# Loading the fourth pair of token tiles by quarters, and three last output transfers from another queue

## The chip, the cores and the metric

The kernel runs on one core of a Trainium2 chip. The metric is the device time of one execution in microseconds (us). Five engines work side by side, each in its own program order: TensorE (PE, with its weight loads as PEld), VectorE (DVE), ScalarE (ACT), GpSimd (POOL) and SyncE (SP). DMA transfers are issued here by SP and by ScalarE, each through a queue of its own (SPq and ACTq in the profile).

## The reference, cut to what matters

```python
a = softmax(phi)                                  # per head, over 32 memory slots
k_m, v_m = a^T k, a^T v
x = softmax(q k_m^T / 8) v_m                      # (2304, 512) after joining the heads
x = ((x @ w_a) * (x @ w_b)) @ w_out               # first MLP, d_ff = 1536
h = x @ w_in                                      # second MLP, (2304, 2048)
g = h * sigmoid(1.702 * h)
out = g @ w_out2                                  # (2304, 512), float32
```

The change touches only the last product, `out = g @ w_out2`, and the transfer of `out` to DRAM.

## The kernel before

The tensor `g` is not kept on the chip: each finished piece goes to a DRAM scratch tensor `g2d` (2048 by 2304, the contraction first) and comes back in the order that the last product wants. That product runs over nine pairs of token tiles (`NW = 9`, 256 tokens a pair). The contraction of 2048 is 16 chunks of 128; a quarter is `K4 = 4` chunks.

**Splitting.** Every operand is split into a high part and a low part, and a product is three matmul passes. A loaded piece of `g` of one token tile and one quarter (128 by 512) is split by one ACT copy (line 308) and one subtraction on DVE or POOL (line 302, `combine`). The result is a block in one of the six `sb_s` slots; in the profile the blocks are `attn` and the loaded pieces are `acc`. PE takes a block in 12 matmuls (line 1335) and with that frees the slot. The chunks of the weight are the `wo2` tiles, which the profile names by the buffers in which they lie (`wv`, `whl_a`, `y`, `g`, `whl_b`, `eff_b`).

**The front.** Pairs 0 to 2 (`NF = 3`) are the front. Their pieces come by quarters, one DMA of 512 KB for one pair and one quarter, into six `f_s` slots (the last two of these are given when the last raw weights are requested). All three pairs advance together, quarter by quarter, over 24 blocks in six PSUM banks. Meanwhile the last rows of `w_out2` are still arriving as `raw` (line 334, SP queue) and are decoded: ACT line 417, DVE lines 419, 423, 427 and 432, ACT line 448 and `combine`. DVE's line 432 frees the `raw` slot for the next load.

**Pairs 3 and 4** (`NS = 5`) follow one after the other, eight blocks each, in quarter order. Their pieces come by halves, one DMA of 1024 KB (line 1204) into one of three `fw_s` slots. These three wide slots lie over the same memory as the six `f_s` slots: the first over the two given last, the second over two others, the third over the remaining two. Two of them are given at the mark `front`, when the last quarter piece has been split, and the third once a block of pair `NF`'s second half has been split. So the halves of pair 3 can't be loaded before the front's last pieces in that memory have been split.

**Pairs 5 to 8** are computed with seven products instead of eight (line 1366). They need combined weights (`blocks`), made between the blocks from pieces of `w2d` that the ACT queue loads (line 1298, two `tb_s` slots).

**The order.** A planner inside the kernel (`Order`) runs these steps as streams with priorities and assumed durations and thereby writes out a fixed order for each engine and each queue. An instruction that waits holds all that stands behind it on its engine. A slot is handed on when the planner emits the instruction that frees it.

**The output.** `store` sends one tile of 128 tokens as four DMAs of 64 KB (line 1417), all from SP. A pair of the last kind has two outputs: `o1` is stored after the product P4 is added, `o0` at the very end, after P3.

Of the kernel before, what the change touches and what calls it, by code (L numbers as in the profile page):

```python
# [56 lines left out]
def crowded():  # L57
    measured()
    Lengths.pool, Lengths.both, Lengths.slow = 1.3, 1.75, 1.55


def short():
    Lengths.dve, Lengths.act, Lengths.psum = 68, 94, 52
    Lengths.pool, Lengths.both, Lengths.slow = 1.0, 1.0, 1.0


def dve(n, fast=False):
    return Lengths.dve + n / (1.92 if fast else 0.96)


def act(n, psum=False):
    return (Lengths.psum if psum else Lengths.act) + n / 1.2
# [102 lines left out]
def tile_mem_attention_moe_moe2(  # L175
# [13 lines left out]
    nc = tc.nc  # L189
# [4 lines left out]
    NT, DM = out.shape  # L194
    F1 = w_o1.shape[0]
    F2 = w_o2.shape[0]
    P = 128
# [5 lines left out]
    QP = P // 4  # L203
# [13 lines left out]
    K4 = F2 // P // 4  # L217
    NB = 2 * P
# [93 lines left out]
    loaded = {}  # L312
# [415 lines left out]
    def give(slots_, views):  # L728
        slots_.free += [[x, now()] for x in views]
# [202 lines left out]
    win_s, hb_s, f_s, fw_s, sb_s, tb_s = Slots(), Slots(), Slots(), Slots(), Slots(), Slots()  # L932
    wo2_t, blocks = {}, []

    def views(m, n, count, o=0):
        return [m[:, o + i * n:o + (i + 1) * n] for i in range(count)]
# [79 lines left out]
    def room_chunks(*flat):  # L1016
        for x in flat:
            od.mark(now(), "room", "o2", len(wo2))
            wo2.append(x.rearrange("p (i f) -> p i f", i=2))
# [4 lines left out]
    def room_last():  # L1024

        short()
        od.handicap[DVE] = W1
        used = wt["o1", NG1 - 1][0]
        room_chunks(*views(g1_m, CN, 3), *views(used, CN, 2), *views(big["eff_b"], CN, 1))
        for x, o, n in (  # L1030
            (big["y0"], 0, 14), (big["y0"], 18 * DM, 3), (eff_m, 0, 4), (attn_m[0], 4 * SN, 1),
            (attn_m[1], 2 * SN, 5), (big["eff_b"], CN, 2), (p2_rest[0], 0, 4),
        ):
            blocks.extend(x.rearrange("p (i f) -> p i f", i=2) for x in views(x, BN, n, o))
        for q in order:
            for j in range(2):
                for u in range(2):
                    yield "mark", "g2", q, j, u
        n = KD * 2 * N2
        give(f_s, views(acc, FN, 1, n + 2 * FN))  # L1040
        give(tb_s, views(acc, 2 * DM, 2))
        for p in range(F2 // P // 2):
            od.spawn(PT, load_pair(p))
        for c, x in enumerate(views(acc, FN, 2, n), len(pieces) - 3):
            yield "mark", "raw", c
            give(f_s, [x])
        t = yield "mark", "wo2", F2 // P - 1
        crowded()
        od.mark(t, "decoded")
        yield "mark", "front"  # L1050
        wide = views(acc, 2 * FN, 3, n)
        give(fw_s, wide[:2])
        yield "mark", "sb", NF, 2 * K4, 0
        give(fw_s, wide[2:])
        for p in range(F2 // P // 2):
            yield "mark", "wt", p
        short()
        give(dm_s, views(acc, DM, 4))
# [133 lines left out]

    NF, NS, NW = 3, 5, NT // NB

    def gated_part(s, i, o, e):
        t = 0.0
        for g in range(o // G2, (e - 1) // G2 + 1):
            for n in range(i * NB // N2, ((i + 1) * NB - 1) // N2 + 1):  # L1200
                for j in range(2):
                    t = max(t, (yield "mark", "g2", (g, n // 2), j, n % 2))
        f = s[0].rearrange("p (c t) -> p c t", c=e - o)
        nc.sync.dma_start(
            out=f, in_=g2d[o * P:e * P, i * NB:(i + 1) * NB].rearrange("(c p) t -> p c t", p=P)
        )
        od.load(max(t + 2500.0, s[1]), 1.7 * (e - o) * P * NB * 4, "f", i, o)
        loaded["f", i, o] = s, f

    def load_gated():  # L1210
        for o in range(0, 4 * K4, K4):
            for i in range(NF):
                s = yield "slot", f_s
                yield from gated_part(s, i, o, o + K4)
        for i in range(NF, NW):
            for o in (0, 2 * K4):
                s = yield "slot", fw_s
                yield from gated_part(s, i, o, o + 2 * K4)

    def split_part(t, src, *key):  # L1220
        b = yield "slot", sb_s
        loaded[key] = b
        od.spawn(4, split_into(max(t, b[1]), b, src, key))

    def split_into(t, b, src, key):
        t = yield from hi_lo(t, b[0][:, HI], b[0][:, LO], src, K4 * P)
        od.mark(t, *key)

    def split_gated():
        for o in range(0, 4 * K4, K4):  # L1230
            for i in range(NF):
                t = yield "mark", "f", i, o
                slot, f = loaded.pop(("f", i, o))
                for s in range(2):
                    yield from split_part(t, f[:, :, s * P:(s + 1) * P], "sb", i, o, s)
                for s in range(2):
                    t = max(t, (yield "mark", "sb", i, o, s))
                f_s.release(slot, t)
        od.mark(t, "front")
        for i in range(NF, NW):  # L1240
            yield from (split_whole(i) if i < NS else sums_gated(i))

    def split_whole(i):
# [47 lines left out]
    def load_pair(p):  # L1291

        t = max((yield "mark", "w2d", 2 * p), (yield "mark", "w2d", 2 * p + 1))
        for x in blocks[4 * p:4 * p + 4]:
            wo2_t.setdefault(p, []).append(x)
        m = yield "slot", tb_s
        x = m[0].rearrange("p (k j f) -> p k j f", k=2, j=2)
        nc.scalar.dma_start(
            out=x.rearrange("p k j f -> p k (j f)"),
            in_=w2d[2 * p * P:(2 * p + 2) * P, :].rearrange("(k p) f -> p k f", p=P),  # L1300
        )
        od.load(max(t, m[1]), 2 * P * DM * 4, "pair", p)
        t = max((yield "mark", "pair", p), (yield "mark", "decoded"))
        b11, b12, b21, b22 = (x[:, k, j] for k in range(2) for j in range(2))
        n = DM // 2
        for i, (dst, in0, in1) in enumerate(
            ((b11, b12, b11), (b12, b22, b12), (b22, b22, b11), (b21, b21, b22))
        ):
            t = yield from combine(t, dst, in0, in1, ALU.subtract, n)
            od.spawn(PT, split_t(t, wo2_t[p][i], dst, p, i))  # L1310
        for i in range(4):
            t = max(t, (yield "mark", "wt", p, i))
        tb_s.release(m, t)
        od.mark(t, "wt", p)
# [61 lines left out]
    def sums_out(i, ps):  # L1376
        x = yield "slot", dm_s
        o0 = yield "slot", dm_s
        o1 = yield "slot", dm_s
        lo, hi = slice(0, NB), slice(NB, 2 * NB)  # L1380
        t = yield "mark", "done", i, "P1"
        t, _ = yield ACT, max(t, x[1]), act(NB, True)
        nc.scalar.activation(out=x[0][:, lo], in_=ps["P1"][0][:, :NB], func=AF.Copy)
        bank_m.release(ps["P1"], t)
        base = max(t, o0[1], o1[1])
        for name, dst, src, last in (
            ("P2", o0[0][:, lo], x[0][:, lo], True), ("P6", x[0][:, hi], x[0][:, lo], True),
            ("P7", x[0][:, lo], x[0][:, hi], True), ("P5", o0[0][:, hi], x[0][:, hi], False),
            ("P5", o1[0][:, hi], x[0][:, lo], True), ("P4", o1[0][:, lo], x[0][:, lo], True),
            ("P3", o0[0][:, hi], o0[0][:, hi], True),  # L1390
        ):
            t = yield "mark", "done", i, name
            base, _ = yield DVE, max(t, base), dve(NB)
            nc.vector.tensor_tensor(out=dst, in0=ps[name][0][:, :NB], in1=src, op=ALU.add)
            if last:
                bank_m.release(ps[name], base)
            if name == "P4":
                dm_s.release(x, base)
                store(2 * i + 1, o1[0])
                dm_s.release(o1, base + 4000.0)  # L1400
        store(2 * i, o0[0])
        dm_s.release(o0, base + 4000.0)

    def proj2_out(t, it, ps):
# [3 lines left out]
        store(it, m[0])  # L1408
        dm_s.release(m, t + 4000.0)

    def store(i, src):

        for t in range(i * P, (i + 1) * P, QP):
            b, r = divmod(t, S)
            e, c = divmod(r // QP, QC // 2)
            dst = out[b * S:(b + 1) * S, :].rearrange("(p c) e -> p c e", c=QC)
            nc.sync.dma_start(out=dst[:, 2 * c + e, :], in_=src[t - i * P:t - i * P + QP, :])

    order = [(0, 0), (1, 0), (0, 1), (1, 1), (0, 2), (1, 2)]
    order += [(g, p) for g in range(2, NG2 - 2) for p in range(NP)]  # L1420
# [11 lines left out]
    def main():  # L1432
# [75 lines left out]
        for i in range(3):  # L1508
            yield "mark", "dm_x", i
        room_projected()  # L1510
        od.spawn(6, load_gated())
        od.spawn(5, split_gated())
        for q in order[1:]:
# [74 lines left out]
```

## Time and profile before

| | |
|---|---|
| runs | 789.92, 791.01, 790.88 us; median 790.88 us |
| profiled execution | 790.42 us |
| its span (first to last instruction or transfer) | 788.6 us |
| granted TensorE clock, mean over the span | 0.996 |
| instructions | 14,299 |

The profiled execution has 1.8 us outside its span and lies 0.46 us below the median of the runs. In the rows below a line begins with its start in us and its length in us; "idle before" is how long the engine had stood and what released it. Matmul starts are reliable, their ends are modelled and overlap the next start.

### The profile page before, as it was taken

The numbers are of one execution on the slowest core, as the hardware profiler recorded it, in microseconds if no ns is written. First come the engines' busy times: TensorE is split into PE (matmuls) and PEld (weight loads), VectorE is DVE, ScalarE is ACT, GpSimd is POOL, SyncE is SP. The second block draws the span as 40 slices with busy tenths as digits, with TensorE's granted clock in tenths as the row PEclk, the third lists the DMA queues.
The fourth block names the chain that finished last, engine by engine and source line by source line (L and its number), as shares of the span: only waits on it lengthen the run. The fifth ranks groups of instructions, "written<-read, shape, count | busy, mean of one in ns | idle before, by whom it ended". The sixth has DMA issues, their size and how long they took to land.

```text
span 788.6 us, 14299 instructions
## 1 busy us (share of the span) xinstructions
PE 772.0 (98%) x5216; PEld 711.6 (90%) x5216; DVE 638.9 (81%) x1135; ACT 417.8 (53%) x925; POOL 365.2 (46%) x343
## 2 busy tenths in 40 slices
PE   8999999999999999999999999999999997999997
PEld 7777789999899899989999999999998885889997
DVE  4888978999999997977989778777867878547886
ACT  4567768564645655445565555555544445434442
POOL 1224225553645644436799655333341046453563
PEclk9999999999999999999999999999999998999999
DMA  8866400122213221230013545455598738624421
GB/s 297 311 190 196 148 25 28 55 81 81 81 54 108 81 81 53 72 90 1 1 65 101 183 159 172 149 164 174 208 309 271 226 135 257 215 75 134 135 81 28
DMA packets 70151, 103.96 MB, mean 132 GB/s; under 512 B 5824, under 2 KB 48832, under 8 KB 70080
## 3 DMA queue, kind: packets, MB, share of 16 engines
q1 hardware_dynamic: 64768, 93.84, 37.3%
q10 hardware_dynamic: 5312, 9.21, 3.3%
q8 instruction: 41, 0.67, 0.4%
q14 instruction: 30, 0.25, 0.1%
HBM read 75.24 MB, written 27.79 MB: 131 GB/s over the span
## 4 chain that ended last, share of the span: by engine, by line
PE 83%; DVE 5%; DMA 4%; ACT 3%; issue 2%; POOL 1%; ACTq 0%; POOLq 0%; DVEq 0%; SPq 0%
PE bank L1135 22%; PE bank L831 18%; PE bank L1366 10%; PE bank L864 10%; PE bank L887 9%; PE bank L1335 6%; PE bank L787 3%; DMA raw<-in_moe_w_out_dram 2%; PE bank L619 1%; PE bank L575 1%; DMA raw<-in_moe_w_b_dram 1%; DVE attn L302 1%; PE bank L756 1%; PE bank L494 1%; DMA acc<-w2d 1%
## 5 line engine op out<-in xcount | busy, mean ns | idle before, releaser
L1177 DVE TENSOR_TENSOR acc<-bank,acc 128x384 f32<-128x384 f32 x168 | 89.7, 553 | 31.8 <-PE bank L1135 20.2
L302 DVE TENSOR_TENSOR attn<-acc,attn 128x512 fp32r<-128x512 f32 (+1 forms) x93 | 88.0, 967 | 30.7 <-ACT attn L308 30.6
L302 POOL TENSOR_TENSOR acc<-acc 128x512 f32<-128x512 f32 (+2 forms) x59 | 76.2, 1306 | 55.7 <-DVE attn L302 30.5
L308 ACT ACTIVATE attn<-acc 128x512 fp32r<-128x512 f32 (+2 forms) x114 | 66.6, 603 | 62.4 <-PE bank L1366 18.7
L1187 ACT ACTIVATE acc<-acc 128x384 f32<-128x384 f32 x96 | 49.3, 523 | 53.1 <-DVE acc L1177 52.2
L844 ACT ACTIVATE gr<-bank 128x288 f32<-128x288 f32 x96 | 38.9, 405 | 64.0 <-PE bank L831 60.9
L302 POOL TENSOR_TENSOR y<-gr,y 128x288 fp32r<-128x288 f32 x40 | 36.3, 908 | 49.9 <-ACT y L308 49.7
L847 DVE TENSOR_TENSOR gr<-bank,gr 128x288 f32<-128x288 f32 x96 | 43.1, 449 | 15.1 <-PE bank L831 8.5
L831 PE MATMUL bank<-attn,eff 128*128 128x288 f32 x384 | 54.4, 296 | 0.0
L831 PEld LDWEIGHTS bank<-attn,eff 128*128 128x128 f32 x384 | 52.1, 188 | 1.3 <-issue 0.9
L864 PE MATMUL bank<-g,whl_b 128*128 128x288 f32 x384 | 52.8, 295 | 0.1
L1135 PE MATMUL bank<-attn,y 128*128 128x384 f32 x288 | 52.3, 335 | 0.0
L864 PEld LDWEIGHTS bank<-g,whl_b 128*128 128x128 f32 x384 | 51.7, 188 | 0.6 <-POOL whl_b L302 0.3
L887 PE MATMUL bank<-y,whl_a 128*128 128x512 f32 (+1 forms) x240 | 51.5, 370 | 0.0
L1335 PE MATMUL bank<-wv,attn 128*128 128x512 f32 x180 | 45.9, 411 | 5.2 <-ACT attn L308 5.2
L1135 PEld LDWEIGHTS bank<-attn,y 128*128 128x128 f32 x288 | 50.1, 188 | 0.0
L419 POOL TENSOR_SCALAR dm<-dm 128x512 f32<-128x512 f32 x21 | 34.7, 1656 | 31.8 <-ACT dm L417 31.7
L887 PEld LDWEIGHTS bank<-y,whl_a 128*128 128x128 f32 x240 | 41.9, 188 | 8.0
L1335 PEld LDWEIGHTS bank<-wv,attn 128*128 128x128 f32 x180 | 35.7, 199 | 13.7 <-ACT attn L308 5.6
L302 POOL TENSOR_TENSOR y<-acc,y 128x256 fp32r<-128x256 f32 (+1 forms) x22 | 19.8, 912 | 59.2 <-ACT y L308 59.2
L302 POOL TENSOR_TENSOR g<-gr,g 128x288 fp32r<-128x288 f32 x28 | 27.0, 966 | 40.8 <-ACT g L308 40.6
L907 DVE TENSOR_TENSOR acc<-bank,acc 128x512 f32<-128x512 f32 (+1 forms) x72 | 38.4, 551 | 5.9 <-PE bank L887 5.2
(269 smaller groups left out, 2022.3 us busy)
## 6 DMA issues: line engine op xcount, KB each, us to landing
g2d<-acc SPq DMA_DIRECT2D x96, 192.0 KB, 2.3
raw<-in_moe_w_out_dram SPq DMA_DIRECT2D x28, 512.0 KB, 4.3
acc<-g2d SPq DMA_DIRECT2D x12, 1024.0 KB, 6.1
raw<-in_moe_w_in_dram SPq DMA_DIRECT2D x16, 512.0 KB, 3.8
acc<-g2d SPq DMA_DIRECT2D x12, 512.0 KB, 5.7
raw<-in_moe_w_a_dram SPq DMA_DIRECT2D x20, 256.0 KB, 2.7
raw<-in_moe_w_b_dram SPq DMA_DIRECT2D x20, 256.0 KB, 3.0
q<-in_q_dram SPq DMA_DIRECT2D x8, 576.0 KB, 6.0
```

The lines of the kernel that those rows point to most:

```text
L302: (nc.gpsimd if e == POOL else nc.vector).tensor_tensor(out=dst, in0=in0, in1=in1, op=op)
L308: nc.scalar.activation(out=hi, in_=src, func=AF.Copy)
L831: nc.tensor.matmul(ps[0][:, :U], e[c][:, sw, i * CW + j * P:i * CW + (j + 1) * P], attn(b, mv, c, u * U, U), start=(n == 0), stop=(n == 3 ...
L844: nc.scalar.activation(out=gr[0], in_=pa_[0][:, :U], func=AF.Copy)
L847: nc.vector.tensor_tensor(out=gr[0], in0=pb[0][:, :U], in1=gr[0], op=ALU.mult)
L864: nc.tensor.matmul(ps[0][:, :U], w[:, sw, j, mb * P:(mb + 1) * P], g1[0][:, j, mv, :], start=(n == 0), stop=(n == 3 * G1 - 1),)
L887: nc.tensor.matmul(ps[0][:, :e - o], w[:, sw, j, mb * P:(mb + 1) * P], g1_all[mv][:, j, o:e], start=(n == 0), stop=(n == 3 * G1 - 1),)
L1135: nc.tensor.matmul(ps[0][:, :N2], w[:, sw, r, :], y[mv][r], start=(n == 0), stop=(n == 5))
L1177: nc.vector.tensor_tensor(out=s[0], in0=ps[0][:, :N2], in1=x[0], op=ALU.add)
L1187: nc.scalar.activation(out=c[0], in_=c[0], func=AF.Gelu_apprx_sigmoid)
L1335: nc.tensor.matmul(ps[i, s][0], b[0][:, sw, c - o, :], wo2[c][:, mv], start=(c == n == 0), stop=(c == 4 * K4 - 1 and n == 2),)
L1366: nc.tensor.matmul(ps[name][0][:, :NB], x[0][:, sw, c, :], moving(b, h // 2 + c, mv), start=(h == c == n == 0), stop=(h > 0 and c == K4 - ...
```

## The change

The fourth pair (`i = 3`) is taken out of the pairs that are loaded by halves and joins the loads by quarters: after the twelve quarters of the front its four quarters follow, through the same `f_s` slots, and its pieces are split by the same stream as those of the front. The mark `front`, which gives two of the wide slots, now comes after these four. The third wide slot now waits for a block of pair 4. The order in which PE's steps are called for is not changed: the front of pairs 0 to 2, then pair 3, then pair 4.

In the last pair the final output tile (`o0`) has three of its four transfers issued by ScalarE and the fourth by SP.

```diff
-        yield "mark", "sb", NF, 2 * K4, 0
+        yield "mark", "sb", NQ, 2 * K4, 0
...
-    NF, NS, NW = 3, 5, NT // NB
+    NF, NQ, NS, NW = 3, 4, 5, NT // NB
...
+    QUARTERS = [(i, o) for o in range(0, 4 * K4, K4) for i in range(NF)]
+    QUARTERS += [(i, o) for i in range(NF, NQ) for o in range(0, 4 * K4, K4)]
+
     def load_gated():
-        for o in range(0, 4 * K4, K4):
-            for i in range(NF):
-                s = yield "slot", f_s
-                yield from gated_part(s, i, o, o + K4)
-        for i in range(NF, NW):
+        for i, o in QUARTERS:
+            s = yield "slot", f_s
+            yield from gated_part(s, i, o, o + K4)
+        for i in range(NQ, NW):
             for o in (0, 2 * K4):
                 s = yield "slot", fw_s
...
     def split_gated():
-        for o in range(0, 4 * K4, K4):
-            for i in range(NF):
-                t = yield "mark", "f", i, o
...
+        for i, o in QUARTERS:
+            t = yield "mark", "f", i, o
...
         od.mark(t, "front")
-        for i in range(NF, NW):
+        for i in range(NQ, NW):
             yield from (split_whole(i) if i < NS else sums_gated(i))
...
-        store(2 * i, o0[0])
+        store(2 * i, o0[0], (nc.sync,) if i < NW - 1 else (nc.scalar, nc.scalar, nc.scalar, nc.sync))
...
-    def store(i, src):
+    def store(i, src, queues=(nc.sync,)):
...
-            nc.sync.dma_start(out=dst[:, 2 * c + e, :], in_=src[t - i * P:t - i * P + QP, :])
+            queue = queues[n % len(queues)]
+            queue.dma_start(out=dst[:, 2 * c + e, :], in_=src[t - i * P:t - i * P + QP, :])
```

## Rows read from the trace of the kernel before

**Rows 1.** The page: busy time and share of the span of each engine.
```profile
PE 772.0 (98%) x5216; PEld 711.6 (90%) x5216; DVE 638.9 (81%) x1135; ACT 417.8 (53%) x925; POOL 365.2 (46%) x343
```

**Rows 2.** Waits of PE from 560 us on: total us, times, longest.
```profile
PE bank L1335 <- ACT attn L308: 5.2, 1, 5.2
```

**Rows 3.** PE in order of time, 580 to 704 us: start, length, what.
```profile
636.23 0.85 PE L1335 MATMUL bank<-eff_b,attn 128*128 128x512 f32 x3
...
650.15 0.86 PE L1335 MATMUL bank<-eff_b,attn 128*128 128x512 f32 x3
656.16 9.87 PE L1335 MATMUL bank<-wv,attn 128*128 128x512 f32 x30 [5.15 <-ACT attn L308]
...
681.14 7.16 PE L1335 MATMUL bank<-wv,attn 128*128 128x512 f32 x30
...
703.40 1.58 PE L1366 MATMUL bank<-y,attn 128*128 128x256 f32 x12
```

**Rows 4.** Windows: busy us of each engine, granted clock, DMA share, GB/s.
```profile
618.00:624.00 6.00, 6.00 (x28) 4.88 (x26) 4.42 (x8) 2.23 (x4) 0.00 (x0) 1.00 0.91 298
624.00:630.00 6.00, 6.00 (x27) 4.88 (x26) 4.83 (x9) 2.61 (x5) 0.00 (x0) 1.00 0.45 133
630.00:643.00 13.00, 13.00 (x58) 10.57 (x57) 12.02 (x18) 6.11 (x15) 6.83 (x7) 1.00 0.11 42
...
656.20:662.00 5.80, 5.80 (x14) 4.51 (x15) 5.45 (x7) 4.04 (x9) 4.09 (x3) 0.50 0.71 228
...
703.00:783.00 80.00, 80.00 (x672) 79.91 (x671) 63.52 (x78) 32.98 (x56) 40.02 (x26) 1.00 0.31 92
```

**Rows 5.** Issues on SP's queue in order of time.
```profile
615.48 0.43 SPq L1204 DMA_DIRECT2D acc<-g2d  x1
619.83 5.26 SPq L334 DMA_DIRECT2D raw<-in_moe_w_out_dram  x2
643.24 1.04 SPq L1204 DMA_DIRECT2D acc<-g2d  x2
...
663.34 1.01 SPq L1204 DMA_DIRECT2D acc<-g2d  x2
```

**Rows 6.** ACT and its queue in order of time.
```profile
629.10 0.67 ACT L417 ACTIVATE acc<-raw 128x512 f32<-128x512 f32 x1 [2.65 <-DMA raw<-in_moe_w_out_dram]
...
655.48 2.19 ACT L308 ACTIVATE attn<-acc 128x512 fp32r<-128x512 f32 x4 [0.49 <-DVE y L302]
```

**Rows 7.** DVE in order of time.
```profile
618.47 0.69 DVE L302 TENSOR_TENSOR attn<-acc,attn 128x512 fp32r<-128x512 f32 x1
...
624.01 0.69 DVE L432 SCALAR_TENSOR_TENSOR dm<-raw,dm 128x512 uint32<-128x512 uint32 x1
624.62 0.69 DVE L302 TENSOR_TENSOR attn<-acc,attn 128x512 fp32r<-128x512 f32 x1
...
631.82 0.68 DVE L302 TENSOR_TENSOR attn<-acc,attn 128x512 fp32r<-128x512 f32 x1
...
633.80 0.69 DVE L302 TENSOR_TENSOR eff_b<-acc,eff_b 128x512 fp32r<-128x512 f32 x1 [0.70 <-ACT eff_b L448]
...
642.53 0.68 DVE L302 TENSOR_TENSOR attn<-acc,attn 128x512 fp32r<-128x512 f32 x1
```

**Rows 8.** Line 1204 (loads of g) from 560 us on: issue to landing.
```profile
DMA to landing us min/median/max: 4.2/5.9/9.9
```

**Rows 9.** POOL in order of time: its last combined weight.
```profile
684.24 0.92 POOL L302 TENSOR_TENSOR rest<-acc,rest 128x256 fp32r<-128x256 f32 x1
```

**Rows 10.** The last addition on DVE; SP's issues from 784.45 us; ACT's first issue.
```profile
783.60 0.42 DVE L1394 TENSOR_TENSOR acc<-bank,acc 128x256 f32<-128x256 f32 x1 [0.97 <-PE bank L1366]
...
784.48 1.79 SPq L1417 DMA_DIRECT2D out_dram<-acc  x4
...
1.18 0.72 ACTq L317 DMA_DIRECT2D phi<-in_phi_dram  x1
```

**Rows 11.** Line 449 (stores of 256 KB from ACT's queue): ns min/median/max.
```profile
L449 ACTq DMA_DIRECT2D w2d<-dm x12: 326/353/538, 562.3 to 629.2; - x12
```

More of the change, by code (lines that the diff above doesn't have):

```diff
@@ L1229, in split_gated @@
     def split_gated():
-        for o in range(0, 4 * K4, K4):
-            for i in range(NF):
-                t = yield "mark", "f", i, o
[L1233 to L1238, printed above, removed]
+        for i, o in QUARTERS:
+            t = yield "mark", "f", i, o
+            slot, f = loaded.pop(("f", i, o))
+            for s in range(2):
+                yield from split_part(t, f[:, :, s * P:(s + 1) * P], "sb", i, o, s)
+            for s in range(2):
+                t = max(t, (yield "mark", "sb", i, o, s))
+            f_s.release(slot, t)
         od.mark(t, "front")
-        for i in range(NF, NW):
+        for i in range(NQ, NW):
             yield from (split_whole(i) if i < NS else sums_gated(i))
@@ L1409, in proj2_out @@
         dm_s.release(m, t + 4000.0)
-    def store(i, src):
-        for t in range(i * P, (i + 1) * P, QP):
+    def store(i, src, queues=(nc.sync,)):
+        for n, t in enumerate(range(i * P, (i + 1) * P, QP)):
             b, r = divmod(t, S)
```

## The prediction, made before the change was run

> **What bounds the kernel.** The page comes first: PE is busy 98% of the span [rows 1], so the change can pay only where PE stands, or at the very end. The list of PE's waits then shows where it stands: from 560 us on there is one wait, 5.2 us, for the ACT instruction that splits a piece of `g` [rows 2]. PE in order of time puts a place to it. The front's last three matmuls start at 650.15 us, the next at 656.16, with 5.15 us idle before it: the first block of pair 3 [rows 3].
>
> Three views say why that block is late. DVE ends the front's last split at 642.53 + 0.68 = 643.21 us [rows 7]. SP issues the two halves of pair 3 at 643.24, at once after it [rows 5]: they lie over the memory of that piece. ACT starts the first split of pair 3 at 655.48 [rows 6], 12.2 us after the issue. Loads of this line took 4.2 to 9.9 us to land [rows 8], so most of the 12 us is the transfer.
>
> The wait costs more than its length. In the window table the granted clock is 0.50 from 656.2 to 662 us and 1.00 in the other windows shown [rows 4]: 1.2 GHz in place of 2.4 after PE had stood. Pair 3 and pair 4 are the same matmuls. Start to start, pair 3 takes 681.14 - 656.16 = 24.98 us, pair 4 takes 703.40 - 681.14 = 22.26 us [rows 3]. The slower clock cost 2.72 us. From 703 to 783 us PE is full [rows 4], so whatever is won before 703 us should reach the end whole.
>
> **The change, part by part.**
>
> *The four quarters of pair 3.* They no longer wait for the front's last split, but take `f_s` slots as these come free. The twelfth quarter went out at 615.48 us [rows 5]. The next slots are the one freed when the eighth quarter is split (618.47 + 0.69 = 619.16 us) and the one given with the second last raw load, at 619.83. Then come the slots of the ninth quarter (624.62 + 0.69 = 625.3) and the tenth (631.82 + 0.68 = 632.5) [rows 5, 7]. So the four should be issued at about 619.2, 620.2, 625.3 and 632.5 us. From 630 to 643 us the DMA engines are 11% busy [rows 4]; even with the longest landing of 9.9 us [rows 8] the last is there by 642.5. Two issues more on SP cost under 0.9 us together (0.43 one [rows 5]), while SP has nothing due.
>
> *The splits of pair 3.* Their number stays. What limits them is `sb_s`: six slots, so block 25 needs block 19 taken by PE. A block is 22.26 / 8 = 2.78 us; the front ends at about 651.0, so block 19 ends near 651.0 - 5 x 2.78 = 637.1 us, and the split of block 25 can start fourteen us before PE wants it. One split is 0.6 us on ACT and 0.7 on DVE [rows 6, 7]. DVE is busy 12.0 of 13 us from 630 to 643 [rows 4], so I put the first splits after 643.2; PE needs the first at 650.8. The margin is 7 us and stays five blocks wide afterwards.
>
> *PE.* Without the wait, block 25 starts one step after the last three matmuls: 650.15 + 3 x 0.23 = 650.84 us (a step is 2.78 / 12). That is 656.16 - 650.84 = 5.32 us earlier. The clock doesn't fall, another 2.72. Gain 8.04 us. The bounds of this term: all of it, or none if the block is as late as before.
>
> *Pair 4.* Its halves now wait for the new mark, and PE wants them at 650.84 + 22.26 = 673.1 us instead of 681.14. Before, they were issued at 663.34 [rows 5], behind the front's output transfers on SP. Block 32 needs block 26 taken (650.84 + 2 x 2.78 = 656.4 us) and some 2 to 4 us of ACT and DVE behind it, so the planner's mark stands for about 659 to 661. SP then has to have passed the front's outputs, which were held up while 2 MB for pair 3 were on their way; that load is gone. Issue at 660, 9.9 us at worst, 0.7 us of ACT: 670.6, in time. Issue at 663.34 as before: 673.9, a wait of 0.8 us. I take no cost and keep 0 to 3 us for the range.
>
> *The combined weights.* POOL ends the last at 684.24 + 0.92 = 685.2 us [rows 9]; PE now wants them at 703.40 - 8.04 = 695.4. Ten us of margin hide eight more splits ahead of them.
>
> *The last raw weights.* The first two quarters add 1 MB just while the last two raw loads come in. The last one is issued at 619.83 + 5.26 - 0.3 = 624.8 us, ACT takes it at 629.10 after waiting for the DMA [rows 5, 6], DVE ends its chunk at 633.80 + 0.69 = 634.49, and PE uses the chunk at 636.23 [rows 3, 7]. The slack is 1.74 us. 1 MB at 298 GB/s takes 3.5 us. From 618 to 624 the engines are 91% busy, which leaves 0.5 us, and from 624 to the issue at 624.8, at 45%, 0.4 us [rows 4]. So at most 2.6 us of quarter traffic is left when the last raw load is issued. If it stood behind all of that, PE would wait 0.9 us; if the two share the engines or its own lead covers the rest, nothing. The bounds are 0 and 0.9 us; I take 0, since 0.9 needs the load's data to begin at its issue, and 4.3 us to landing against 1.8 us of transfer says that they don't.
>
> The Trainium skill, DMA: Bandwidth & Descriptors, section Queues, rings and completion order, says that each DMA engine consumes the descriptors of one queue in ring order. Raw loads and quarters share SP's queue, so by that rule the upper bound is the one to take, and the sum would be 0.9 us worse. No row here separates standing in line from sharing.
>
> *The last output.* DVE ends at 783.60 + 0.42 = 784.02 us. SP is still issuing `o1` and begins the four of `o0` at 784.48; they take 1.79, so the last starts at about 785.84 [rows 10]. Now SP has one, at 784.48, and ACT, idle, begins at about 784.1. One issue on ACT is 0.33 us at least, 0.35 in the middle [rows 11], and 0.72 at the start of the span [rows 10]; SP's pitch for the same transfer is 0.45. With 0.45 ACT's third starts at 785.0 and the end moves 0.84 us. The bounds are 0.3 us (0.72 each) and 1.1 (0.33 each). I take 0.84, since the transfer is the same.
>
> **Sum.** Profiled execution 790.42 - 5.32 - 2.72 - 0.84 = 781.54 us. It lies 0.46 us below the median of the runs, 790.88, so the forecast is 782.0 us.
>
> **The rivals.**
>
> *The wait moves to pair 4.* Pair 4 becomes the first pair that waits for wide slots, and SP must come past the outputs in its queue first. For it: its halves went out at 663.34, and PE now wants them 8 us earlier. Against it: what held SP then was the traffic for pair 3, and pair 3's data are now on the chip 30 us before. It decides from an issue at 662.5 us on. At 663.3 to 665.5 it costs 0.8 to 3 us: 782.8 to 785.0 us.
>
> *The wait stays.* The splits of pair 3 stand on ACT or DVE behind work that waits for the combined weights' loads, and block 25 is as late as before. For it: both engines run in program order, and that work lies between the splits. Against it: the splits have the better priority, and the margin is 7 us. Then only the output edit pays: 790.88 - 0.84 = 790.0 us.
>
> *Slower: the last raw load behind a waiting quarter.* If the planner writes the fourth quarter ahead of the last raw load on SP, that load goes out after the tenth quarter's split, at 632.6 in place of 624.8, with 1.8 us of transfer ahead of it: 9.6 us late, less the slack of 1.74, a wait of 7.9 us at 636 us. PE would stand longer than in the wait above, after which the clock fell, so 2.7 more. 782.0 + 7.9 + 2.7 = 792.6 us. It turns to a loss from a wait of 8.88 - 2.72 = 6.2 us on. Against it: the last raw load's slot is freed by DVE at 624.01, ahead of the ninth quarter's second split at 624.62 and well ahead of the tenth's [rows 7], and the planner hands slots on in that order.
>
> *A small one.* Raw loads strictly in line and a slightly worse order of the decoding: 0.5 to 1.5 us at 636 us, 782.5 to 783.5.
>
> **How the numbers follow.** Forecast as summed 0.72 (781.3 to 783.0), small wait in the front 0.08, wait moved to pair 4 0.11, wait stays 0.05, slower 0.04. The range 781.2 to 785.2 leaves out the last two cases, about 0.04 of the pair 4 case and some 0.05 at the edges. A change of 0.2%, 1.6 us, is about what the runs can tell from none; the first three cases are faster by far more (0.91), the fourth lies within (0.05), the fifth beyond (0.04).
>
> **What the new profile would show.** Right: no wait of PE between 640 and 700 us, the granted clock at 1.00 throughout, four quarter issues of line 1204 between 619 and 633 us, the first matmul of pair 3 near 650.8 and of pair 5 near 695.4, three output issues on ACT's queue, PE's end near 775.5. Wrong: a PE wait near 636 (raw weights), near 651 (splits held up), or near 673 us with the halves of pair 4 issued after 662.5; or ACT's output issues far apart.

## The result, and the profile after

Four runs of the changed kernel took 783.01, 782.08, 781.91 and 782.08 us, median 782.08, against 790.87 for the kernel before on the same chip: a ratio of 0.9894 (95% interval 0.9877 to 0.9911), 7.0 to 9.7 us less. The forecast was 782.0 us. In two later sets of runs, in which the kernel before took 789.8 and 789.5 us in the median, the change measured 0.9908 (0.9895 to 0.9922) and 0.9907 (0.9890 to 0.9923), some 7.3 us less; the sections below say where the difference lies.

The profiled execution is the longest of the four, 783.01 us with a span of 781.2. PE's waits from 560 us on, after the change: total, times, longest. This answers to [rows 2]; the wait of 5.2 us is gone, and another, of 0.2 us, is there for a chunk of weights.

```profile
PE bank L1336 <- DVE eff_b L302: 0.2, 1, 0.2
```

PE in order of time, after, with the matmuls that answer to [rows 3]:

```profile
636.70 0.42 PE L1336 MATMUL bank<-eff_b,attn 128*128 128x512 f32 x1
637.34 0.72 PE L1336 MATMUL bank<-eff_b,attn 128*128 128x512 f32 x2 [0.22 <-DVE eff_b L302]
...
651.12 0.85 PE L1336 MATMUL bank<-eff_b,attn 128*128 128x512 f32 x3
651.80 7.03 PE L1336 MATMUL bank<-wv,attn 128*128 128x512 f32 x30
...
673.93 7.16 PE L1336 MATMUL bank<-wv,attn 128*128 128x512 f32 x30
...
696.20 1.58 PE L1367 MATMUL bank<-y,attn 128*128 128x256 f32 x12
```

Pair 3 follows the front one step after it, and the 30 matmuls that took 9.87 us take 7.03. Pair 3 lasts 673.93 - 651.80 = 22.13 us (24.98 before), pair 4 takes 22.27 (22.26). The eff_b matmul that stood at 636.23 stands at 636.70: this execution came 0.47 us late to that place. At 602 us it was already 0.45 us late (the first matmuls of `whl_a` start at 602.73 instead of 602.28), ahead of the first quarter of pair 3. The next step is 0.64 us instead of 0.23, a loss of 0.41.

The windows of the loading, after (columns as in [rows 4]):

```profile
618.00:624.00 6.00, 6.00 (x28) 4.87 (x27) 4.26 (x9) 2.42 (x5) 0.00 (x0) 1.00 0.97 333
624.00:630.00 6.00, 6.00 (x27) 4.88 (x26) 4.17 (x8) 2.33 (x4) 0.00 (x0) 1.00 1.01 343
...
656.00:662.00 6.00, 6.00 (x28) 4.90 (x27) 2.98 (x4) 2.54 (x6) 4.74 (x6) 1.00 0.56 174
```

The granted clock is 1.00 where it was 0.50, and the DMA engines are full from 618 to 630 us, where 133 GB/s flowed in the second half before. SP's issues, after, beside [rows 5]:

```profile
616.21 4.12 SPq L1204 DMA_DIRECT2D acc<-g2d  x2
620.55 0.35 SPq L334 DMA_DIRECT2D raw<-in_moe_w_out_dram  x1
620.95 0.42 SPq L1204 DMA_DIRECT2D acc<-g2d  x1
625.65 0.35 SPq L334 DMA_DIRECT2D raw<-in_moe_w_out_dram  x1
626.21 6.23 SPq L1204 DMA_DIRECT2D acc<-g2d  x2
...
663.98 11.33 SPq L1204 DMA_DIRECT2D acc<-g2d  x3
```

The first quarter of pair 3 stands ahead of the second last raw load (it is the second of the two from 616.21 on), the second quarter between the two raw loads, the other two behind both: the order that the prediction read off the slots. ACT, after, at the first split of pair 3 and at the first of pair 4:

```profile
646.33 0.63 ACT L308 ACTIVATE attn<-acc 128x512 fp32r<-128x512 f32 x1 [0.51 <-issue]
...
671.20 2.20 ACT L308 ACTIVATE attn<-acc 128x512 fp32r<-128x512 f32 x4 [2.33 <-DVE attn L302]
```

The first is 5.5 us ahead of PE's first use at 651.80, the second 2.7 us ahead of 673.93. The end, after, beside [rows 10]:

```profile
776.39 0.42 DVE L1395 TENSOR_TENSOR acc<-bank,acc 128x256 f32<-128x256 f32 x1 [0.98 <-PE bank L1367]
...
776.85 1.47 ACTq L1419 DMA_DIRECT2D out_dram<-acc  x3
...
778.00 0.32 ACTq L1419 DMA_DIRECT2D out_dram<-acc  x1
```

From the end of the last addition (776.81) to the end of the span are 781.2 - 776.81 = 4.39 us (the tail, from here on); before it was 788.6 - 784.02 = 4.58. The third issue from ScalarE begins at 778.00, though the second has ended at 777.25 + 0.43 = 777.68.

In sum the span is 7.4 us shorter: pair 3 starts 656.16 - 651.80 = 4.36 us sooner, lasts 2.85 less, and the tail is 0.19 shorter; pair 4 and the pairs after it take what they took.

### The profile page after: what moved, and what is told of

It is laid out like the page before. It is cut to its first block, busy times and chain, and to the rows that moved or that the text cites. A ratio compares the mean times of both kernels' runs of the same rounds, so it can differ in the third digit from the quotient of the medians.

```text
span 781.2 us, 14295 instructions
## 1 busy us (share of the span) xinstructions
PE 768.4 (98%) x5216; PEld 708.7 (91%) x5216; DVE 638.7 (82%) x1132; ACT 416.9 (53%) x924; POOL 369.6 (47%) x347
## 4 chain that ended last, share of the span: by engine, by line
PE 92%; DVE 3%; DMA 2%; ACT 1%; issue 1%; POOL 1%; SPq 0%; ACTq 0%; DVEq 0%; POOLq 0%
PE bank L1135 22%; PE bank L831 18%; PE bank L1336 14%; PE bank L1367 10%; PE bank L864 10%; PE bank L887 10%; PE bank L787 3%; DMA phi<-in_phi_dram 1%; PE bank L619 1%; PE bank L575 1%; DMA kv<-in_v_dram 1%; PE bank L756 1%; PE bank L494 1%; ACT et L547 0%; DVE mx L541 0%
## 5 line engine op out<-in xcount | busy, mean ns | idle before, releaser
L302 DVE TENSOR_TENSOR attn<-acc,attn 128x512 fp32r<-128x512 f32 (+2 forms) x94 | 90.7, 987 | 25.0 <-ACT attn L308 25.0
L302 POOL TENSOR_TENSOR acc<-acc 128x512 f32<-128x512 f32 (+2 forms) x63 | 81.0, 1299 | 46.1 <-DVE attn L302 24.2
L1336 PE MATMUL bank<-wv,attn 128*128 128x512 f32 x180 | 43.0, 393 | 0.0
L417 ACT ACTIVATE dm<-raw 128x512 f32<-128x512 f32 x41 | 27.0, 667 | 28.3 <-DMA raw<-in_moe_w_b_dram 12.3
```

The costliest lines, as they stand in the source:

```text
L302: (nc.gpsimd if e == POOL else nc.vector).tensor_tensor(out=dst, in0=in0, in1=in1, op=op)
L1336: nc.tensor.matmul(ps[i, s][0], b[0][:, sw, c - o, :], wo2[c][:, mv], start=(c == n == 0), stop=(c == 4 * K4 - 1 and n == 2),)
```

## The experiments

The two theories at the start: PE's wait and the slow clock behind it are what the quarters save (8 us), and the output edit gives 0.8; or the output edit gives only the 0.2 us of the profile above.

**The quarters alone, and the output edit alone.** The first is the change with `store(2 * i, o0[0])` as it was; the second is the kernel before with the `store` of the change and

```diff
-        store(2 * i, o0[0])
+        store(2 * i, o0[0], (nc.sync,) if i < NW - 1 else (nc.scalar, nc.scalar, nc.scalar, nc.sync))
```

> The quarters without the output edit: all four transfers of the last tile from SP again. Theory from the trace after the change: the output edit moved the end by only some 0.2 us against the last addition (4.58 us from its end to the end of the span before, 4.39 after), so this should take about 782.3 us, and the tail goes back to about 4.6 us. Rival, the term as forecast (0.84 us): 782.9 us. PE's waits as after the change in both.

> The output edit alone on the kernel before: the wait of 5.15 us ahead of pair 3 and the slow clock behind it must be there as before. Theory (the output edit is worth 0.2 us): about 790.7 us. Rival (0.84 us as forecast): 790.0 us. If the two edits did not simply add up, the sum of the gains of this run and of the quarters alone would differ from 8.8 us by more than 0.5.

The quarters alone: 782.32 us, 0.9910 (0.9894 to 0.9926) of the kernel before, which took 789.22 on this chip. That is the 782.3 that the theory of 0.2 us expected, with a tail of 780.2 - 775.74 = 4.46 us, and no slower than both edits together in their three sets of runs (782.1 to 782.4). The output edit alone: 788.15 us, 0.9985 (0.9974 to 0.9997). Both expected times were missed there, since they were worked out from 790.9 us for the kernel before. PE, the last addition on DVE and ACT's queue in its profile:

```profile
656.79 8.60 PE L1335 MATMUL bank<-wv,attn 128*128 128x512 f32 x30 [4.94 <-ACT attn L308]
...
782.96 0.42 DVE L1394 TENSOR_TENSOR acc<-bank,acc 128x256 f32<-128x256 f32 x1 [0.98 <-PE bank L1366]
...
783.41 1.31 ACTq L1417 DMA_DIRECT2D out_dram<-acc  x3
```

The wait of 4.9 us is where it was, and the tail is 787.1 - 783.38 = 3.72 us, 0.86 less than before. So the edit can give the forecast 0.84 where it stands alone, and on top of the quarters it gives nothing that the runs show. The two gains, 6.9 and 1.1 us, add up to 8.0, which is 0.8 short of 8.8 and beyond the 0.5 named in the expectation; but the 8.8 was taken against a kernel before at 790.87, so this sum alone doesn't tell whether the edits add up. What took the 0.84 in the changed kernel came out with the last three runs.

**The quarters held back until the last raw load is requested.**

```diff
         for i, o in QUARTERS:
+            if i >= NF:
+                yield "mark", "raw", len(pieces) - 1
             s = yield "slot", f_s
```

> The change, but the four quarters of pair 3 may be requested only once the last raw load has been requested, so that no quarter is ahead of the last two raw loads in SP's queue. Theory: the step of 0.64 us in place of 0.23 between PE's matmuls near 637 us after the change comes from that traffic (raw landing 7.3 and 6.7 us instead of 4.3). Then the landings go back to about 4.3 us, PE's wait near 637 us is gone, pair 3 still starts without a wait, and the time falls by 0.4 us to about 781.7. Rival: the late chunk comes from the changed order of the decoding on DVE and ACT, or the held quarters now come late for pair 3: a PE wait near 637 or near 651 us remains and the time is 782.1 or more.

781.26 us, 0.9897 (0.9880 to 0.9915), below the 781.7 expected; the tail is shorter here too (3.66 us). The time from issue to landing of line 334 from 600 us on in the changed kernel (first), then SP's issues and the same time in this one:

```profile
DMA to landing us min/median/max: 4.4/5.6/7.3
```

```profile
620.47 4.60 SPq L334 DMA_DIRECT2D raw<-in_moe_w_out_dram  x2
625.16 7.70 SPq L1204 DMA_DIRECT2D acc<-g2d  x4
...
DMA to landing us min/median/max: 4.1/4.6/5.7
```

The last two raw loads land after 4.1 and 4.2 us instead of 7.3 and 6.7, PE waits nowhere from 500 us on, and pair 3 starts at 651.00. The quarters, all four requested only from 625.16 on, are still in time. So the late landings were the traffic of the quarters. PE's wait shows this less well: in all six profiles with quarters ahead of the raw loads these land late (5.6 to 7.3 us and 5.0 to 6.7 us), and in four of them PE doesn't wait for the chunk.

**The wait kept, but filled with matmuls.** In the kernel before:

```diff
+                for _ in range(20 if (i, o, s) == (NF, 0, 0) else 0):
+                    nc.tensor.matmul(ps[i, s][0], wo2[0][:, HI, :P], wo2[0][:, HI], start=True, stop=True)
                 for c in range(o, o + K4):
```

> The kernel before, with 20 extra matmuls of the same size (20 x 0.231 = 4.6 us) on PE in the wait ahead of pair 3; their sums are overwritten by pair 3's first matmul. Nothing comes sooner. Theory: of the 8.04 us, 2.72 are the clock alone. The wait for the first split shrinks to under 1 us, the granted clock stays 1.00, pair 3 still starts near 656.2 us but takes 22.3 us instead of 25.0, and the time is 790.87 - 2.7 = 788.2 us. Rival: pair 3 is slow because its splits arrive slowly, not because of the clock: it still takes 25 us with waits between its blocks, and the time stays at 790.9 us.

787.31 us, 0.9985 (0.9970 to 1.0000): by the runs no gain is shown. Nine of the twelve lie between 786.7 and 788.0, three at 790.7 to 791.2. The three have a mean granted clock of 0.997, the nine one of 0.999 or 1.000: in the three PE was at the lower clock for some time again. Where, and what made the rest of the difference, is open, for the profile is of one of the nine (786.83 us). In it the theory holds. PE in order of time, and a window:

```profile
650.79 4.72 PE L1334 MATMUL bank<-wv 128*128 128x512 f32 x20
655.35 2.95 PE L1337 MATMUL bank<-wv,attn 128*128 128x512 f32 x12
```

```profile
656.00:662.00 6.00, 6.00 (x27) 4.91 (x27) 5.97 (x7) 4.22 (x10) 4.69 (x5) 1.00 0.64 190
```

With PE kept busy the clock stays at 1.00 behind the same wait, and pair 3 takes 677.52 - 655.35 = 22.17 us.

**Only the order changed.** In the trace of the kernel before the first half of pair 3, issued at 643.24, landed after 7.5 us, at 650.7. From then until 655.44 ACT was with the combined weights, and with one copy of a finished bank (line 293), which stand ahead of the split in its program order: it split three pieces of the weights, stood from 652.27 to 653.63 ahead of a load of line 1298, and issued a second one at 655.07. The load's time from issue to landing, and ACT in order of time, before:

```profile
DMA to landing us min/median/max: 7.5/7.5/7.5
```

```profile
651.85 0.42 ACT L308 ACTIVATE y<-acc 128x256 fp32r<-128x256 f32 x1 [0.45 <-DVE acc L302]
653.63 0.42 ACTq L1298 DMA_DIRECT2D acc<-w2d  x1
654.09 0.42 ACT L308 ACTIVATE y<-acc 128x256 fp32r<-128x256 f32 x1 [1.83 <-DVE y L302]
654.41 0.58 ACT L293 ACTIVATE acc<-bank 128x512 f32<-128x512 f32 x1
655.07 0.37 ACTq L1298 DMA_DIRECT2D acc<-w2d  x1
```

This is the kernel before, pair 3 by halves, with the combined weights written behind its first splits:

```diff
         t = max((yield "mark", "pair", p), (yield "mark", "decoded"))
+        if p > 1:
+            t = max(t, (yield "mark", "sb", NF, 0, 1))
```

> The kernel before, pair 3 still by halves, but the work on the combined weights from the third pair of chunks on is written behind the first splits of pair 3. Theory: the first half of pair 3 landed 7.5 us after its issue, at 650.8, and the last 4.7 us of PE's wait are ACT standing at the two loads of line 1298, which wait for combined weights. Then ACT starts the first split near 651, PE waits under 1.5 us, the granted clock stays 1.00, pair 3 takes 22.3 us, and the time falls by 6 to 7.5 us to some 782 to 784. Rival, as the prediction read it (the transfer itself ends the wait): PE still waits some 4 to 5 us, and the time stays within 2 us of the kernel before.

784.16 us, 0.9936 (0.9923 to 0.9949) of 789.77, where the changed kernel took 782.32. By the ratio that is 5.1 us less (4.0 to 6.1), where 6 to 7.5 were expected. PE's wait ahead of pair 3, and ACT in order of time:

```profile
651.30 7.42 PE L1337 MATMUL bank<-wv,attn 128*128 128x512 f32 x30 [0.42 <-ACT attn L308]
```

```profile
642.51 0.90 ACTq L1298 DMA_DIRECT2D acc<-w2d  x2
643.51 1.58 ACT L293 ACTIVATE dm<-bank 128x512 f32<-128x512 f32 x3 [3.85 <-DVE attn L302]
650.61 2.19 ACT L308 ACTIVATE attn<-acc 128x512 fp32r<-128x512 f32 x4 [5.53 <-DMA acc<-g2d]
```

Here ACT does wait for the load, until 650.61, and PE's wait is 0.42 us instead of 5.15. The granted clock stays at 1.00, and pair 3 takes 673.82 - 651.30 = 22.52 us. The rest behind the changed kernel: pair 5 starts 0.63 us later (696.08 against 695.45 in the changed kernel's profile on this chip), pairs 5 to 8 take 0.72 us more, the tail 0.45.

**The kernel before, a second profile.**

> The kernel before once more, for a second profile. On one chip its runs spread from 787.0 to 791.4 us, those of every kernel without the wait ahead of pair 3 by 0.5 us. Theory: the wait is there each time, but the time that PE spends at the lower clock behind it differs: the first 30 matmuls of pair 3 took 9.87 us in one profile, 8.60 in another with the same wait. This profile should have a wait of about 5 us and some other length between 7.2 and 14 us for the 30, and its total should follow that. Rival: the spread comes from the stages before, and the 30 matmuls take 9.9 us again whatever the total.

788.23 us in the one run. PE in order of time, ACT's queue and engine ahead of the first split of pair 3, and windows:

```profile
655.21 8.63 PE L1335 MATMUL bank<-wv,attn 128*128 128x512 f32 x30 [4.28 <-ACT attn L308]
...
678.95 7.17 PE L1335 MATMUL bank<-wv,attn 128*128 128x512 f32 x30
```

```profile
652.69 0.40 ACTq L1298 DMA_DIRECT2D acc<-w2d  x1
653.14 0.42 ACT L308 ACTIVATE y<-acc 128x256 fp32r<-128x256 f32 x1 [1.81 <-DVE y L302]
653.46 0.58 ACT L293 ACTIVATE acc<-bank 128x512 f32<-128x512 f32 x1
654.12 0.37 ACTq L1298 DMA_DIRECT2D acc<-w2d  x1
654.53 2.19 ACT L308 ACTIVATE attn<-acc 128x512 fp32r<-128x512 f32 x4 [0.49 <-DVE y L302]
```

```profile
655.20:658.40 3.20, 3.19 (x8) 2.47 (x9) 2.85 (x3) 3.20 (x7) 2.43 (x2) 0.50 0.89 314
658.60:664.00 5.40, 5.40 (x25) 4.40 (x24) 5.40 (x8) 3.23 (x9) 4.50 (x4) 1.00 0.53 122
```

The wait is 4.28 us, the clock is back after some 3.3 us instead of 6, and pair 3 takes 23.74 us: the clock cost 1.5 us here, 2.7 in the first profile, 1.5 in that of the output edit alone. The expectation holds. 0.9 us of wait and 1.2 of clock are most of the 2.2 us between the two profiled executions of the kernel before (790.42 and 788.23). The other runs fit this: of the 23 of the kernel before on one chip, the eleven with a mean granted clock of 0.995 took 789.9 us in the median, the nine with 0.997 took 788.4.

**The changed kernel again, and the outputs two and two.** The second kernel holds the quarters back as above and has `(nc.scalar, nc.scalar, nc.sync, nc.sync)`.

> The changed kernel once more, beside the others on one chip, where the quarters alone took 782.32 us and the held quarters 781.26. Theory: the 0.22 us that PE waited for the last weight chunk in the first profile, and the end of 4.39 us behind the last addition, are what that one execution had; the other profiles with the output edit ended 3.7 us behind the last addition. So the median here lies between the two: 781.3 to 781.7 us, and the tail is 3.7 us. Rival: both are in every execution, and the median is 782.1 or more.

> The held quarters (none requested ahead of the last raw load), and the last tile's four transfers two from ScalarE and two from SP. Theory: with three on ScalarE the third is the last to land (issue pitch 0.45 us and landings of 1.9 to 2.2 us there, 1.7 from SP); two and two end the issues about 0.3 us sooner. 781.0 us against 781.26 with held quarters and three and one. Rival: the queues interleave and the landings stretch by as much: 781.3 us.

The changed kernel: 782.32 us, tail 780.4 - 776.07 = 4.33 us, no wait of PE. So for the tail the rival is right (4.3 us is in this kernel's executions); the wait for the last chunk comes in some of them only. Two and two: 781.23 us, 0.9894 (0.9879 to 0.9909), tail 779.5 - 775.89 = 3.61 us against 3.66 with three and one: no difference that can be told.

**More instructions on ACT.** What differs between the tail of 4.3 us and those of 3.7 is the hole before the third issue. Two kernels write ACT's copy of the product P1 three times, in the last pair (two instructions more) or in the last four (eight more):

```diff
+        for _ in range(3 if i == NW - 1 else 1):
-        nc.scalar.activation(out=x[0][:, lo], in_=ps["P1"][0][:, :NB], func=AF.Copy)
+            nc.scalar.activation(out=x[0][:, lo], in_=ps["P1"][0][:, :NB], func=AF.Copy)
```

> The changed kernel with two more ACT instructions in the last pair (the copy of P1 written three times), some 14 us before the end and with ACT idle behind them. In both profiles of the changed kernel the third transfer from ScalarE is issued 0.32 us after the second has been, and lands 2.1 to 2.2 us later; with the output edit on the kernel before and with held quarters it followed at once and landed after 1.7 to 1.8 us. Theory: the hole belongs to the place of that instruction in ACT's stream, so two instructions more move it; then the end comes 3.7 us behind the last addition instead of 4.3, and the time falls by 0.6 us against the changed kernel beside it. Rival: the hole belongs to the transfers (their state when ScalarE issues them); then nothing changes.

> The same with the copy of P1 written three times in each of the last four pairs: eight more ACT instructions. By the theory of the place in ACT's stream the hole is gone here too or stands before another issue; the tail is 3.7 us where no hole stands between the three issues. By the rival the hole of 0.32 us and the late landing are there as in the changed kernel. The time follows the tail: 0.6 us less than the changed kernel beside it, or the same.

> The changed kernel, beside these two on one chip: 782.1 to 782.3 us, with the hole of 0.32 us ahead of the third issue from ScalarE and a tail of 4.3 to 4.4 us in the profile, if these are in every execution; 781.3 to 781.7 us and a tail of 3.7 if they are not.

Two more: 781.93 us, 0.9903 (0.9888 to 0.9917) of 789.45. Eight more: 781.46 us, 0.9896 (0.9881 to 0.9910). The changed kernel beside them: 782.40 us. ACT's queue with two more (first fence: the first issue, then the second and third) and with eight more:

```profile
775.59 0.36 ACTq L1420 DMA_DIRECT2D out_dram<-acc  x1
...
776.27 0.81 ACTq L1420 DMA_DIRECT2D out_dram<-acc  x2
```

```profile
776.44 1.31 ACTq L1420 DMA_DIRECT2D out_dram<-acc  x3
```

With two more instructions the hole (0.32 us) stands one issue earlier, between the first and the second, and the tail is still 4.25 us: the expected 3.7 was missed there. With eight more there is none, and the tail is 780.1 - 776.40 = 3.70. The changed kernel has it ahead of the third again (tail 4.43). The tails explain 0.2 of the 0.5 us that the kernel with two more is ahead of the changed kernel beside it, and 0.7 of the 0.9 us with eight more; the rest is not shown. The hole moves with the place in ACT's stream and does not belong to the transfers.

The traces say where that place is. Counted with its semaphore waits, the instruction behind the hole is number 1216 on ACT's sequencer in all four executions that have the hole (by this count two more instructions shift the stream by one place, since one semaphore wait fewer stands in the trace, and eight more by five). With eight more, and with the output edit alone, number 1216 stands 9 us and more ahead of the first issue; with held quarters it is the first of the three issues, for which ACT had stood 8 us anyway. The profile has an instruction queue, q14, whose packets are 8 KB each. One of them moves 0.7 to 1.1 us behind number 1216 in the four executions, and 7 us and more ahead of the first issue in the three without a hole. So the hole comes with the loading of ACT's further instructions; that the loading causes it is likely, but no run varied it by itself.

## Why the prediction was right, and where it was not

- **Place and mechanism.** The wait ahead of pair 3 and the clock behind it are gone, pair 3 follows the front at once, and nothing behind it gives the gain back. That was the forecast, and the time is within 0.1 us of it, in the set of runs where the kernel before took 790.87. Against a kernel before at 789.5 to 789.8 the same change saves 7.3 us: the saving is as large as what the kernel before loses, and that differs from execution to execution (wait 4.3 to 5.2 us, clock 1.5 to 2.7). The sum was made from the costliest of three profiles. That it met the median to 0.1 us is in part luck. In the profile the three terms came to 7.40 us instead of 8.88 and nothing cancelled that; but the profiled execution, at 783.01, lies 0.93 us above the median of its four runs, and the kernel before's lay 0.46 below its own.
- **The wait (5.32 us).** In the profile 4.36: this execution came 0.47 us later to the front's end for reasons ahead of the change, and 0.41 are lost at 637 us.
- **What ended the wait: wrong.** The prediction put "most of the 12 us" from issue to first split down to the transfer. The transfer took 7.5 of them and landed at about the moment PE wanted it. The rest was ACT's program order: the work on combined weights, with two loads of line 1298, stood ahead of the splits. With the order alone changed, PE's wait fell to 0.42 us without any earlier load. The row was there: the releaser of the first split is `DVE y` [rows 6], a combined weight, not the load; the list of waits names only ACT. The forecast survived because in the changed kernel the first split also stands earlier in ACT's order: from 640 us on it has two issues of that line ahead of it (644.48 and 645.86) instead of four, and it starts at 646.33.
- **The rival that the wait stays** named that mechanism and was given 0.05 on the margin of 7 us; the measured margin was 4 to 5.5 us (split begun at 646.33 and finished on DVE near 647.7, wanted at 651.8).
- **The clock (2.72 us).** 2.85 in the profile. The run with filled wait separates it from the wait: pair 3 as fast as pair 4 with nothing sooner. That its runs show no sure gain leaves the size open, not the mechanism in the profile.
- **The last raw weights (0, bounds 0 and 0.9).** The load did come late, as standing in line would have it and against the reason for taking 0: in the first profile 2.5 us later (6.7 to landing instead of 4.2), in the five others with the quarters not held 0.8 to 2.1, where the bound was 2.6. PE waited for the chunk in two of the six (the first and third of the changed kernel, 0.2 us each, a loss of 0.41 and 0.50 us) and not in the other four, where the slack was enough. The Trainium skill, DMA: Bandwidth & Descriptors, section Queues, rings and completion order, has the descriptors of a queue consumed in ring order on each DMA engine. Here the trace is in line with it: raw loads and quarters landed in the order of their issue (second last raw load 627.9, quarter 630.7, last raw load 632.4, quarter 633.5).
- **Pair 4.** The wait did not move there, but by less than the prediction had it: its halves were issued at 663.98, behind the 662.5 named as the turning point, and landed in 6.4 us instead of the 9.9 assumed. ACT's first split was 2.7 us ahead of PE.
- **The last output (0.84 us).** 0.19 in the profile. The term is right where no hole stands between ScalarE's issues (0.86 to 0.92 in three profiles: the output edit alone, held quarters, eight more instructions); the changed kernel has a hole of 0.32 us ahead of the third, which also lands after 2.1 to 2.2 us instead of 1.7 to 1.8. That ScalarE's three issues would follow each other without a hole was assumed, not read.

The version with held quarters is ahead of both kernels, at 781.26 us (781.16 to 781.70 over six runs) against 782.1 to 782.4 for the changed kernel, measured in different sets of runs; some 0.7 us of that is the tail without the hole, which its ACT order happens to have.

## What to carry to other kernels

When a wait is put down to an engine, read what that engine itself waited for just before: a load that is 7.5 us of a 12 us delay may have landed in time, and the rest be other work, with DMA issues of its own, that stands in front of it in program order. A gap of 4.3 to 5.2 us on PE cost its length and then 1.5 to 2.7 us through the lower clock, and the second part varied from run to run; gaps of 0.2 to 0.4 us cost no clock here. Loads that are brought forward go ahead of something in their queue: hold them behind the last transfer that the next stage is waiting for, if there is time to spare.

## What the hardware showed that was not expected

Three issues in a row from ScalarE had a hole of 0.32 us whose place moved by one issue when two instructions were added ahead of it, and that was absent with eight; the issues just behind it landed after 2.1 to 2.4 us instead of 1.7 to 2.0. It stands ahead of the same instruction of ACT each time, number 1216, and an instruction packet of 8 KB moves about 1 us later. The time at the lower clock after nearly the same wait (4.3 to 5.2 us) was some 3.3 us in one execution and 6 in another; the kernels in which pair 3 starts without a wait and PE is not filled spread over 0.3 to 1.5 us from run to run, over four to six runs each; the kernel before spread over 4.3 us in 23 runs on one chip (787.02 to 791.35) and over 2.2 us in nine and in seven runs on two others.
